# Marking accumulating banks with work that is there anyway, in a one-core attention and mixture-of-experts kernel

## The chip, the cores and the metric

The kernel runs on one core of a Trainium2 chip. A core has a matrix engine (TensorE, PE in the profile, with its weight loads as PEld), a vector engine (VectorE, DVE), an activation engine (ScalarE, ACT), a general engine (GpSimd, POOL) and a queue engine for transfers (SyncE, SP). Each runs its own list of instructions in order; they wait for each other through semaphores. Matrix products land in PSUM, eight banks of 128 partitions by 512 fp32 values. The metric is the device time of one execution in microseconds (us).

## The reference, cut to what matters

Two stages. Cross attention between tokens x and 32 state rows per head gives 8 × (512 + 32) = 4352 rows of 512 values. These go through eight experts, all of them on every row, weighted by a matrix P that a gate and eight rounds of row and column normalisation produce.

```python
def _moe_ref(x, w_gate, w1, w2) -> np.ndarray:
    ...
    logits = x @ w_gate
    logits = logits - logits.max()
    P = np.exp(logits)
    for _ in range(8):
        P /= P.sum(1, keepdims=True) + 1e-09
        P /= P.sum(0, keepdims=True) + 1e-09
        P *= N / E
    out = np.zeros((N, D), dtype=np.float32)
    for e in range(E):
        h = np.maximum(x @ w1[e], 0.0)
        ye = h @ w2[e]
        out += P[:, e:e + 1] * ye
    return out.astype(np.float32)
```

Here D is 512, the hidden width 1024, E is 8.

## The kernel before, in words

**Two parts.** The first 135 us are a list of some 736 small operations (`PLAN`, issued one by one by `issue`): attention, the gate, the normalisation rounds, expert 0 whole, and the start of expert 1. After it comes a loop over `work`, the pairs of expert e = 1 to 7 and row block bi = 0 to 8 (eight blocks of 512 rows, one of 256); the document counts iterations from 0. Iteration 0 is expert 1, block 0, whose hidden layer the list has made already. Nothing is reordered afterwards: every engine takes its instructions as the program text issues them.

**One iteration** is three generators advanced in turns. `layer2(e, bi, i)` makes the second layer of the block. `layer1` of the next block makes its hidden layer in eight pieces: two matmuls of 512 columns into one of four banks (`hps`, pool "h"), a relu by ScalarE, and after the fourth and eighth piece four sums by VectorE (lines 281 to 284). `project`, in some iterations, makes V, the projected first-layer weights, for blocks to come: a "session" of line 235, which starts in the E bank and in one of the two accumulating banks.

**The second layer** multiplies 2 × 2 blocks with seven products in place of eight (Strassen's way, Winograd's form), each of eight matmuls of 256 columns (line 334). The document numbers them 1 to 7 as `layer2` issues them: A; E; B; A; B; E; B, where the letters are PSUM banks. Each but the first is followed by its add: VectorE reads the bank and adds it, weighted by P, to `acc` (line 348, two instructions). Bank B begins as a copy of A by ScalarE (line 363), and products 3, 5 and 7 accumulate onto it. So products 5 and 7 may begin only when VectorE has read what was in the bank before.

**The marker.** Products accumulate onto data that ScalarE wrote. [...] The banks stay the same tiles for the whole loop (`seeds`, used in turns by the iteration's parity).

**Scaling.** `acc` holds expert 0's output unweighted. `weigh` (lines 294 and 296) multiplies a block of rows by its column of P; iteration 0 does the first four row blocks ahead of product 1, on VectorE, ScalarE, VectorE and GpSimd.

**The step counter.** `step()` is called after each turn of `layer2` and each piece of `layer1`; each sixth call advances `load_w` of the next expert by one, from block 1 on. `load_w` issues four weight loads, idles for ten turns, and then makes eight subtractions of weights on VectorE (line 206), which land wherever the counter puts them among the adds and sums. What is left at block 6 is done at once.

The loop's turn:

```python
        for k in range(7):
            next(l2)
            step()
            ...
            for _ in range(pat[k]):
                next(l1, None)
                step()
```

Of the kernel before, what the change touches and what calls it, by code (L numbers as in the profile page):

```python
# [9 lines left out]
FP32 = mybir.dt.float32  # L10
FP16 = mybir.dt.float16
# [37 lines left out]
704V 689P 693P 690P 730P 398V 694A 399P 733P 731V 691A 732A 735A 734A 400V  # L49
""".split()  # L50
ENGINES = {"P": "PE", "V": "DVE", "A": "ACT", "G": "POOL", "D": "DMA", "S": "SPQ", "H": "HOST"}
NT_ = 2
ETX = 0
POOLB = 1
# [47 lines left out]
            slot.users.append(self)  # L102


def issue(ops):
    for step in PLAN:
        op = ops[int(step[:-1])]
        assert all(d.end for d in op.after) and ENGINES[step[-1]] in op.on
        for slot in op.takes:
            slot.ring.taken.append(slot)  # L110
            slot.tile = slot.make()
        op.emit(ENGINES[step[-1]])
        op.end = True
    assert all(op.end for op in ops) and len(PLAN) == len(ops)
# [3 lines left out]
def kernel(  # L118
# [9 lines left out]
    nc = tc.nc  # L128

    B, H, S, D = x.shape  # L130
# [14 lines left out]
    DH = Dm // 2  # L145
# [15 lines left out]
    def bank(shape, dtype, name, tag="bank"):  # L161
        return pools[tag].tile(shape, dtype, name=name, tag=tag)

    aT = persist.tile([128, B, NQ, S], FP16, name="aT")
# [5 lines left out]
    identh = persist.tile([128, 128], FP16, name="identh")  # L170
# [87 lines left out]
    hid = {}  # L258
    late = []
    final = (E - 1, B)  # L260
    seeds = []

    def layer1(e, bi):

        t0, tn = blocks[bi]
        th = tn // 2
        Hm = hpool.tile([128, 2, NJ, S], FP16, name="Hm", tag="Hm")
        sm = hpool.tile([128, 3, NJ, S // 2], FP16, name="sm", tag="sm")
        hid[(e, bi)] = (Hm, sm)
        for j in range(NJ):  # L270
            for i in range(2):
                fb = i * NJ + j
                hps = bank([128, S], FP32, "hps", "h")
                hidden_ps(e, bi, fb, hps[:, :tn])
                nc.scalar.activation(out=Hm[:, i, j, :tn], in_=hps[:, :tn], func=AF.Relu)  # L275
                if j % 2 and i and (e, bi) != final:
                    def sums(jj=ds(j - 1, 2)):
                        a11, a21 = Hm[:, 0, jj, :th], Hm[:, 0, jj, th:tn]
                        a12, a22 = Hm[:, 1, jj, :th], Hm[:, 1, jj, th:tn]
                        s1, s2, s4 = (sm[:, k, jj, :th] for k in range(3))  # L280
                        nc.vector.tensor_add(s1, a21, a22)  # L281
                        nc.vector.tensor_sub(a21, a11, a21)  # L282
                        nc.vector.tensor_sub(s2, s1, a11)  # L283
                        nc.vector.tensor_sub(s4, a12, s2)  # L284

                    if DEFER and bi == 0 and j == 1:
                        late.append(sums)
                    else:
                        sums()
                yield  # L290

    def weigh(k, eng):
        if eng == "ACT":
            nc.scalar.mul(acc[:, k, :], acc[:, k, :], Pmat[:, k, 0:1])
        else:
            (nc.vector if eng == "DVE" else nc.gpsimd).tensor_scalar(
                out=acc[:, k, :], in0=acc[:, k, :], scalar1=Pmat[:, k, 0:1], scalar2=None, op0=ALU.mult)
# [22 lines left out]
    def layer2(e, bi, n):  # L320
        t0, tn = blocks[bi]
        nk = tn // 256
        th = tn // 2
        Hm, sm = hid.pop((e, bi))
        w2h, T = w16[e][1], tsum[e]
        tb = t0 // 128
        p = Pmat[:, :, e:e + 1]
        A = bank([128, 2, DH], FP32, "A", "A")
        Eb = bank([128, 2, DH], FP32, "E", "E")

        def product(dst, lhs, rhs, first=False):
            for c in range(nk):
                for j in range(NJ):
                    nc.tensor.matmul(dst[:, c], lhs(j, c), rhs[:, j],  # L334
                                     start=first and c == 0 and j == 0, stop=(j == NJ - 1),
                                     skip_group_check=True)

        def h(i, half):
            return lambda j, c: Hm[:, i, j, ds(half * th + c * 128, 128)]

        def s(k):
            return lambda j, c: sm[:, k, j, ds(c * 128, 128)]

        def add(src, row, col):
            for c in range(nk):
                k = tb + row * nk + c
                dst = acc[:, k, ds(col * DH, DH)]
                nc.vector.scalar_tensor_tensor(out=dst, in0=src[:, c], scalar=p[:, k], in1=dst,  # L348
                                               op0=ALU.mult, op1=ALU.add)

        def seed(i):
            bb = bank([128, 2, DH], FP32, "Bseed", "B%d" % i)
            nc.tensor.matmul(bb.rearrange("p c d -> p (c d)"), identh, aT[:, 0, 0], start=True, stop=True)
            seeds.append(bb)

        if not n:
            for k, eng in enumerate(("DVE", "ACT", "DVE", "POOL")):
                weigh(k, eng)
        product(A, h(0, 0), w2h[:, :NJ, :DH], True)
        if not n:  # L360
            seed(0)
        Bb = seeds[n % 2]
        nc.scalar.copy(out=Bb[:, :nk], in_=A[:, :nk])  # L363
        yield
        product(Eb, s(0), T[:, 0], True)
        if not n:
            seed(1)
        add(Eb, 1, 1)
        yield
        product(Bb, s(1), T[:, 1])  # L370
        add(Bb, 0, 1)
        yield
        product(A, h(1, 0), w2h[:, NJ:, :DH])
        add(A, 0, 0)
        yield
        product(Bb, h(0, 1), T[:, 2])
        add(Bb, 1, 1)
        yield
        product(Eb, s(2), w2h[:, NJ:, DH:])
        add(Eb, 0, 1)  # L380
        yield
        product(Bb, h(1, 1), T[:, 3])
        add(Bb, 1, 0)
        if e == E - 1 and bi < B:
            for k in range(2 * nk):
                nc.sync.dma_start(out=outx[bi][:, k, :], in_=acc[:, tb + k, :])
        yield


    ops = []  # L390
# [96 lines left out]
    for g in range(4):  # L487
# [10 lines left out]
        t = op((0, 1, g), {"PE": (0.35, 0.55)}, turn, bd[g // 2 * 2:g // 2 * 2 + 2] + [makeh], [ps])  # L498
# [68 lines left out]
    for b in range(B):  # L567
# [5 lines left out]
        for g in range(2 if b < NT else 0):  # L573
# [11 lines left out]
            t = op((due_x(2 * b + g) - 2.0, 0), {"PE": (0.70, 0.88)}, turnX, [x_ready[b][g], makeh], [ps], [xn[b]])  # L585
# [221 lines left out]
    def tile_of(tag, shape):  # L807
# [6 lines left out]
    c = sk({"DVE": (0.36, 0.48)}, lambda: nc.vector.reduce_max(  # L814
        out=tile_of("lmx", [128, 1]), in_=logits.rearrange("p t e -> p (t e)"), axis=AX_X), gates)
    mT = psum([1, 128], FP32, "mT_ps")
    c = sk({"PE": (0.11, 0.35)}, lambda: nc.tensor.transpose(mT.tile, sm_["lmx"], ident32), [c, make32], takes=[mT])
# [3 lines left out]
    c = sk({"PE": (0.18, 0.45)}, lambda: nc.tensor.matmul(gb.tile, ones128[0:1, :], sm_["gm"]), [c], takes=[gb])  # L821
# [193 lines left out]

                op((due_1 + 5.0 * bi, 2, j), {"DVE": (1.70, 1.85)}, sums, kept[-4:]).goal = -0.9

    issue(ops)
    for e in range(2):
        w16[e] = (wslots[e][0].tile, wslots[e][1].tile)  # L1020
    hpool = pools1["h"]
# [6 lines left out]
    n = 0  # L1028

    def step():  # L1030
        nonlocal n
        n += 1
        if n % 6 == 0 and wload:
            try:
                next(wload[0])
            except StopIteration:
                wload.pop(0)
# [4 lines left out]
    for i, (e, bi) in enumerate(work):  # L1042
        if bi == 1 and e + 1 < E:
            wload.append(load_w(e + 1))
        if (e, bi) == final:
            layer2_last()
            break
        v, pat = iter(()), PATS if bi == B else PATN if bi == B - 1 else PAT0
        soon = work[:i + (3 if bi == B - 1 else 2)]
        need = sum(b < B for _, b in soon) * (F // 512)  # L1050
        if halves and all_halves - len(halves) < need:
            v, pat = project(halves[:SESSION], i), PATV
            del halves[:SESSION]
        if i:
            next(v, None)
        l2 = layer2(e, bi, i)
        l1 = layer1(*work[i + 1]) if i + 1 < len(work) and work[i + 1] not in hid else iter(())
        for k in range(7):
            next(l2)
            step()  # L1060
            if k == 0:
                next(v, None)
                next(v, None)
            if late:
                late.pop()()
            if e == 1 and bi < B and 3 <= k < 7:
                m = blocks[bi + 1][0] // 128 + k - 3
                if m < NTB:
                    weigh(m, "ACT")
# [3 lines that stand above are left out]
        for part in (l1, l2):  # L1073
            for _ in part:
                pass
        if bi == len(blocks) - 3:
            for _ in (x for w in wload for x in w):
                pass
            wload.clear()
# [30 lines left out]
```

## Time and profile before

| | |
|---|---|
| median of 3 runs | 752.74 us (752.53 to 753.22) |
| profiled execution | 752.75 us |
| its span, first to last instruction | 751.0 us |
| granted TensorE clock, mean over the span | 0.995 |
| PE busy | 736.0 us (98%) |
| DVE busy | 617.0 us (82%) |
| ACT busy | 517.7 us (69%) |
| POOL busy | 70.8 us (9%) |
| chain that ended last: PE / DVE | 92% / 3% |
| products of the second layer (line 334) in the chain | 48% |
| first-layer pieces (line 255) in the chain | 28% |

The span is cut into what each engine does; busy shares overlap. The chain is followed back from the last instruction, at each step to what released it, so its shares add up to the span. A matmul's length in a row includes its way through the array, and the next one starts before it ends; what one costs is read from start to start.

### The profile page before, as it was taken

Reading aid. Unit: us, or ns where it says so; the run is one execution under the profiler, and the core shown is the slowest. Engines: PE = TensorE matmul, PEld = TensorE weight load, DVE = VectorE, ACT = ScalarE, POOL = GpSimd, SP = SyncE. Lnnn points to the kernel's source line nnn. Section 1 sums busy time; section 2 is a strip of 40 time slices with the busy share of each in tenths; the row PEclk is TensorE's granted clock in tenths of the full one; section 3 lists DMA queues with packets and bytes.
Section 4 is the critical chain, followed back from the end, with each engine's and each line's share of the span. In section 5 each row is a group of like instructions: output and inputs, shape, how many; then the busy total and the mean of one; then the engine's idle time right before and its main releaser. Section 6 shows DMA issues by size and latency. Waiting matters only on the chain.

```text
span 751.0 us, 16151 instructions
## 1 busy us (share of the span) xinstructions
PE 736.0 (98%) x6517; PEld 502.2 (67%) x6517; DVE 617.0 (82%) x1529; ACT 517.7 (69%) x1014; POOL 70.8 (9%) x81
## 2 busy tenths in 40 slices
PE   5999999999999999999999999999999999999997
PEld 3444445666777777776776767776777767767776
DVE  5899989877888789788888788887897888887885
ACT  6876856799876766667666766667666676667662
POOL 4674410200010000100000000100001000000000
PEclk9899999999999999999999999999999999999999
DMA  9997560600033000700007000330007000002234
GB/s 179 140 134 131 82 99 1 109 6 1 1 61 53 2 1 2 113 1 2 1 2 112 2 1 1 58 57 1 1 2 112 2 1 2 1 31 94 103 113 141
DMA packets 51323, 36.71 MB, mean 49 GB/s; under 512 B 25392, under 2 KB 43824, under 8 KB 51248
## 3 DMA queue, kind: packets, MB, share of 16 engines
q0 software_dynamic: 22272, 20.97, 18.5%
q1 hardware_dynamic: 27744, 14.18, 7.6%
q8 instruction: 51, 0.84, 0.5%
q10 hardware_dynamic: 1232, 0.52, 0.3%
q14 instruction: 24, 0.20, 0.1%
HBM read 42.48 MB, written 8.91 MB: 68 GB/s over the span
## 4 chain that ended last, share of the span: by engine, by line
PE 92%; DVE 3%; DMA 1%; ACT 1%; POOL 1%; issue 0%; SPq 0%; POOLq 0%; DVEq 0%; ACTq 0%
PE hps L255 28%; PE Bseed L334 20%; PE A L334 14%; PE E L334 14%; PE yps L935 6%; PE hps L897 4%; PE v_ps L235 4%; DMA xT<-x_nat 1%; DMA x_nat<-in_x_dram 1%; PE y L312 0%; PE v_ps L870 0%; POOL a L670 0%; ACT Hm L275 0%; DVE acc L348 0%; POOL E L662 0%; PE su_ps L758 0%
## 5 line engine op out<-in xcount | busy, mean ns | idle before, releaser
L275 ACT ACTIVATE Hm<-hps 128x512 f16<-128x512 f32 (+1 forms) x496 | 265.8, 577 | 130.5 <-PE hps L255 128.1
L255 PE MATMUL hps<-aT,V 128*128 128x512 f16 x880 | 230.6, 379 | 0.0
L334 PEld LDWEIGHTS <-Hm 128*128 128x128 f16 x1888 | 181.6, 98 | 71.3 <-issue 15.9
L348 DVE SCALAR_TENSOR_TENSOR acc<-Bseed,Pmat,acc 128x256 f32<-128x256 f32 x354 | 155.0, 477 | 9.8 <-PE Bseed L334 6.9
L334 PEld LDWEIGHTS <-sm 128*128 128x128 f16 x1416 | 138.3, 98 | 34.5 <-issue 0.3
L334 PE MATMUL A<-w2h,Hm 128*128 128x256 f16 x944 | 123.7, 273 | 0.0
L334 PE MATMUL Bseed<-T,Hm 128*128 128x256 f16 x944 | 123.3, 273 | 0.0
L255 PEld LDWEIGHTS <-V 128*128 128x128 f16 x880 | 86.1, 98 | 50.8
L348 DVE SCALAR_TENSOR_TENSOR acc<-E,Pmat,acc 128x256 f32<-128x256 f32 x236 | 103.2, 476 | 13.8 <-PE E L334 13.5
L281 DVE TENSOR_TENSOR sm<-Hm 128x512 f16<-128x512 f16 (+1 forms) x122 | 50.1, 411 | 60.4 <-ACT Hm L275 60.2
L243 ACT CAST V<-v_ps 128x512 f16<-128x512 f32 x144 | 74.2, 612 | 0.0
L348 DVE SCALAR_TENSOR_TENSOR acc<-A,Pmat,acc 128x256 f32<-128x256 f32 x118 | 51.9, 479 | 17.9 <-PE A L334 17.6
L935 PE MATMUL yps<-w2h,hT 128*128 128x512 f16 x272 | 64.1, 379 | 0.1
L334 PE MATMUL E<-w2h,sm 128*128 128x256 f16 x472 | 61.7, 273 | 0.0
L334 PE MATMUL E<-T,sm 128*128 128x256 f16 x472 | 61.6, 273 | 0.0
L334 PE MATMUL Bseed<-T,sm 128*128 128x256 f16 x472 | 61.5, 272 | 0.0
L363 ACT COPY Bseed<-A 128x512 f32<-128x512 f32 (+1 forms) x62 | 34.1, 550 | 37.9 <-PE A L334 35.3
L282 DVE TENSOR_TENSOR Hm<-Hm 128x512 f16<-128x512 f16 (+1 forms) x122 | 50.3, 412 | 4.2
L284 DVE TENSOR_TENSOR sm<-Hm,sm 128x512 f16<-128x512 f16 (+1 forms) x122 | 50.2, 412 | 4.2
L283 DVE TENSOR_TENSOR sm<-sm,Hm 128x512 f16<-128x512 f16 (+1 forms) x122 | 49.4, 405 | 0.0
L194 POOL DMA_DIRECT2D w1h<-in_moe_w_dram x12 | 8.5, 714 | 396.9 <-PE hps L255 396.5
L935 PEld LDWEIGHTS <-hT 128*128 128x128 f16 x272 | 25.4, 99 | 28.9 <-issue 1.8
(127 smaller groups left out, 617.7 us busy)
## 6 DMA issues: line engine op xcount, KB each, us to landing
w1h<-in_moe_w_dram POOLq DMA_DIRECT2D x16, 512.0 KB, 7.0
w2h<-in_moe_w_dram POOLq DMA_DIRECT2D x16, 512.0 KB, 8.4
out_dram<-acc SPq DMA_DIRECT2D x32, 256.0 KB, 2.5
x_nat<-in_x_dram POOLq DMA_DIRECT2D x16, 256.0 KB, 5.6
st_st<-in_state_dram ACTq DMA_DIRECT2D x1, 256.0 KB, 4.9
st_st<-in_state_dram SPq DMA_DIRECT2D x1, 256.0 KB, 4.2
ETs<-E SPq DMA_TRANSPOSE x16, 4.3
out_dram<-acc SPq DMA_DIRECT2D x4, 64.0 KB, 1.8
```

The source lines that it names most:

```text
L235: nc.tensor.matmul(ps[q][ds(j * Ns, Ns), :], stT[ds(r, 64), bi, q, ds((j ^ q) * Ns, Ns)], w1h[ds(r, 64), 2 * q + j // 2, cols], tile_posit ...
L243: nc.scalar.copy(out=dst, in_=src)
L255: nc.tensor.matmul(out, lhs, rhs, start=(k == 0), stop=(k == len(terms) - 1))
L275: nc.scalar.activation(out=Hm[:, i, j, :tn], in_=hps[:, :tn], func=AF.Relu)
L281: nc.vector.tensor_add(s1, a21, a22)
L282: nc.vector.tensor_sub(a21, a11, a21)
L283: nc.vector.tensor_sub(s2, s1, a11)
L284: nc.vector.tensor_sub(s4, a12, s2)
L334: nc.tensor.matmul(dst[:, c], lhs(j, c), rhs[:, j], start=first and c == 0 and j == 0, stop=(j == NJ - 1), skip_group_check=True)
L348: nc.vector.scalar_tensor_tensor(out=dst, in0=src[:, c], scalar=p[:, k], in1=dst, op0=ALU.mult, op1=ALU.add)
L363: nc.scalar.copy(out=Bb[:, :nk], in_=A[:, :nk])
L935: nc.tensor.matmul(yps.tile, hT[fb].tile[:, ds(tk * 128, 128)], w2h[:, fb, :], start=(fb == 0), stop=(fb == NFB - 1))
```

## The change

Iteration 0 no longer issues the two markers. The first B bank is lent to the first piece of the next block's hidden layer, which is therefore issued right behind product 1, ahead of product 2; the relu reads it from there, and then ScalarE copies A over it. The second B bank is first written by the projection session of iteration 1. ScalarE's scaling of row block 1 moves behind its copy of A, and VectorE scales row block 2 before row block 0. The turn that issues the lent piece calls `step()` once more. `issue` gets a hook for idle matmuls with an empty table.

```diff
+IDLE = {}
...
-def issue(ops):
+def issue(ops, idle):
...
+        idle(op.takes[0].tile if op.takes else None, IDLE.get(int(step[:-1]), 0))
...
-    def layer1(e, bi):
+    def layer1(e, bi, lent=None):
...
-                hps = bank([128, S], FP32, "hps", "h")
+                if lent is None:
+                    hps = bank([128, S], FP32, "hps", "h")
+                else:
+                    hps, lent = lent, None
...
-        def seed(i):
-            bb = bank([128, 2, DH], FP32, "Bseed", "B%d" % i)
-            nc.tensor.matmul(bb.rearrange("p c d -> p (c d)"), identh, aT[:, 0, 0], start=True, stop=True)
-            seeds.append(bb)
-
         if not n:
-            for k, eng in enumerate(("DVE", "ACT", "DVE", "POOL")):
+            for k, eng in ((2, "DVE"), (3, "POOL"), (0, "DVE")):
                 weigh(k, eng)
         product(A, h(0, 0), w2h[:, :NJ, :DH], True)
+        Bb = seeds[n % 2]
         if not n:
-            seed(0)
-        Bb = seeds[n % 2]
+            yield
         nc.scalar.copy(out=Bb[:, :nk], in_=A[:, :nk])
+        if not n:
+            weigh(1, "ACT")
         yield
         product(Eb, s(0), T[:, 0], True)
-        if not n:
-            seed(1)
         add(Eb, 1, 1)
...
+        if not i:
+            seeds += [bank([128, 2, DH], FP32, "Bseed", "B%d" % k) for k in range(2)]
         l2 = layer2(e, bi, i)
-        l1 = layer1(*work[i + 1]) if i + 1 < len(work) and work[i + 1] not in hid else iter(())
+        l1 = iter(())
+        if i + 1 < len(work) and work[i + 1] not in hid:
+            l1 = layer1(*work[i + 1], None if i else seeds[0].rearrange("p c d -> p (c d)"))
+        if not i:
+            next(l2)
+            next(l1)
+            step()
         for k in range(7):
             next(l2)
             step()
```

More of the change, by code (lines that the diff above doesn't have):

```diff
@@ L1016, with idle @@
                 op((due_1 + 5.0 * bi, 2, j), {"DVE": (1.70, 1.85)}, sums, kept[-4:]).goal = -0.9
-    issue(ops)
+    def idle(t, n):
+        if not n:
+            return
+        t = t.rearrange({2: "p a -> p a", 3: "p a b -> p (a b)", 4: "p a b c -> p (a b c)"}[len(t.shape)])[:, :128]
+        for _ in range(n):
+            if t.dtype == FP16:
+                nc.tensor.transpose(t, identh, identh)
+            else:
+                nc.tensor.matmul(t, identh, identh, start=True, stop=True, skip_group_check=True)
+    issue(ops, idle)
     for e in range(2):
```

## The prediction

> **What bounds the kernel now.** First the page's head and its chain of waits: which engine sets the end.
>
> ```profile
> PE 736.0 (98%) x6517; PEld 502.2 (67%) x6517; DVE 617.0 (82%) x1529; ACT 517.7 (69%) x1014; POOL 70.8 (9%) x81
> ...
> PE 92%; DVE 3%; DMA 1%; ACT 1%; POOL 1%; issue 0%; SPq 0%; POOLq 0%; DVEq 0%; ACTq 0%
> ```
>
> TensorE carries 92% of the chain, and from 135 us on it is never idle (77.00 of 77.00 us busy in the stretch 135 to 212). There a microsecond counts only if TensorE issues less, or has to wait. So next the timeline of the loop's first iteration, where the edit lies. Columns: start, length, engine, line, operation, tiles.
>
> ```profile
> 134.73 1.62 ACT L419 CAST V<-v_ps 128x512 f16<-128x512 f32 x3
> 135.14 1.05 PE L334 MATMUL A<-w2h,Hm 128*128 128x256 f16 x8
> 136.03 0.38 PE L353 MATMUL Bseed<-aT,identh 128*128 128x512 f16 x1
> 136.24 0.73 ACT L294 ACTIVATE acc<-acc,Pmat 128x512 f32<-128x512 f32 x1
> 136.41 1.03 PE L334 MATMUL E<-T,sm 128*128 128x256 f16 x8
> 136.86 0.60 ACT L363 COPY Bseed<-A 128x512 f32<-128x512 f32 x1
> 137.28 0.38 PE L353 MATMUL Bseed<-aT,identh 128*128 128x512 f16 x1
> 137.49 0.59 PE L255 MATMUL hps<-aT,V 128*128 128x512 f16 x2
> 137.93 1.04 PE L334 MATMUL Bseed<-T,sm 128*128 128x256 f16 x8
> ```
>
> Starts, not lengths, give TensorE's cost: eight matmuls of 256 columns take 0.87 us (139.23 to 140.10 in the same timeline), four of 512 columns 0.87 us (140.10 to 140.97), so 0.217 us each. A marker thus costs 0.217 us, not 0.38. After the first marker TensorE also waits: product 2 could start at 136.25 but does at 136.41, just behind the last eviction of V (134.73 + 1.62 = 136.35).
>
> Last the timeline of a later iteration with a subtraction of load_w (line 206) in it:
>
> ```profile
> 545.89 0.42 DVE L284 TENSOR_TENSOR sm<-Hm,sm 128x512 f16<-128x512 f16 x1
> 546.24 0.87 DVE L348 SCALAR_TENSOR_TENSOR acc<-Bseed,Pmat,acc 128x256 f32<-128x256 f32 x2
> 546.30 1.03 PE L255 MATMUL hps<-aT,V 128*128 128x512 f16 x4
> ...
> 547.02 0.41 DVE L206 TENSOR_TENSOR T<-w2h 128x512 f16<-128x512 f16 x1
> 547.16 1.04 PE L334 MATMUL Bseed<-T,Hm 128*128 128x256 f16 x8
> 547.36 0.87 DVE L348 SCALAR_TENSOR_TENSOR acc<-E,Pmat,acc 128x256 f32<-128x256 f32 x2
> 548.14 0.41 DVE L281 TENSOR_TENSOR sm<-Hm 128x512 f16<-128x512 f16 x1
> 548.28 0.37 PE L235 MATMUL v_ps<-w1h,stT 64*32 64x512 f16 x1
> ```
>
> Product 7 accumulates into the bank that VectorE has just read for product 5's add (line 348). That add ends at 547.11 and product 7 starts at 547.16: VectorE has no room here. The same holds at the projection session (line 235), which takes the E bank: the E add ends at 548.22, the session starts at 548.28.
>
> **The change part by part.** It has two effects, and the second is not visible in the diff's words.
>
> (1) The first iteration. Two markers leave, 0.43 us of TensorE. Piece 1 takes the first one's place: two matmuls from 136.03 to 136.46. It needs the first half of V (evicted by 135.31), not the last. Product 2 follows at 136.46, past the 136.41 that held it, so this wait (0.16 us) goes too; it ends at 137.33, piece 2 at 137.77. Now product 3 waits for ScalarE: piece 1's second matmul starts 136.25 and lasts 0.38, to 136.63; the relu starts some 0.07 later (after a piece ends it took 0.04 and 0.11 here) and lasts 0.60, to 137.30; the copy of A overwrites the bank the relu read, so it starts at about 137.35 and lasts 0.57 to 0.60. Product 3 starts at about 137.97, 0.04 later than before, but one piece (0.43 us) is already done. Net −0.39. What is late next would be product 5 or 7, but the fourth piece and its sums come 0.4 us earlier too, so nothing new binds. Ends: −0.59 (both markers and the wait go, ScalarE hides) and −0.07 (piece 1 has to wait for V's last eviction, product 3 at 138.3).
>
> ScalarE's scaling (0.73 us) now stands behind its copy; queued behind it is the relu of piece 2, ending about 139.2. Its bank is asked for again by piece 6, near 141.9, and the scaled row by VectorE's second add of product 3, near 139.5: no cost. VectorE scales block 2 before block 0 (the E add wants 2 first, at 137.6): no cost. GpSimd's scaling stays first on its queue, and the weight loads behind it wait for buffers, 396.5 us in all, not for the loop's program order: no cost. The idle hook issues nothing, its table being empty; the built program has two matmuls fewer on TensorE, so the markers do leave.
>
> (2) The step counter. The first iteration now calls step() 16 times, not 15, and every sixth call drives load_w. From there on each subtraction of line 206 is put one step earlier on VectorE. In the built program's order 24 of the 48 get another neighbour. Of these, 12 pass an add that nobody is short of (product 5 starts 0.75 us or more behind product 3's add where this happens; the bank that product 7's add reads is wanted again two iterations later).
>
> Six (before: 196.01, 293.94, 370.94, 468.94, 547.02, 645.11) go from behind product 5's add to ahead of it, behind the sums of lines 281 to 284. Price of one subtraction in a VectorE queue that is full: four in a row, whose rows start at 297.43 and whose follower starts at 298.77, 1.34 / 4 = 0.335 us.
>
> ```profile
> 297.43 0.75 DVE L206 TENSOR_TENSOR T<-w2h 128x512 f16<-128x512 f16 x2
> 298.10 0.75 DVE L206 TENSOR_TENSOR T<-w2h,T 128x512 f16<-128x512 f16 x2
> 298.77 0.87 DVE L348 SCALAR_TENSOR_TENSOR acc<-E,Pmat,acc 128x256 f32<-128x256 f32 x2
> ```
>
> I take 0.325, since the step from a sum to the subtraction replaces one to the add (0.35). Product 7 starts this much later, less its room over the 0.05 release: the add ended 0.12 before product 7 at 371.14 and 469.14, 0.05 to 0.06 at the other four. So 2 × 0.26 and 4 × 0.32 = 1.80. But four of these iterations precede a session which today already waits for the E add that this subtraction delays: its first matmul comes 0.289, 0.290, 0.347, 0.344 us after the last, against 0.203 where there is no wait, 0.46 in all. The E add ends as before, TensorE now arrives later, so this wait is absorbed: 1.80 − 0.46 = +1.34.
>
> Six others (206.28, 284.28, 382.31, 460.22, 558.39, 635.39) go from behind the E add to ahead of it. A session follows at four (206.67, 284.61, 382.64, 635.78), where the E add ends 0.31, 0.24, 0.25 and 0.30 before it. The same subtraction in the same place cost the session 0.087 where the room was 0.3 and 0.143 where it was 0.25 (the four excesses above): 2 × 0.087 + 2 × 0.143 = +0.46. The other two feed product 2, which has over 0.6 us of room.
>
> Sum: −0.39 + 1.34 + 0.46 = +1.41. The profiled execution took 752.75 (span 751.0 and 1.75 around it), like the median, 752.74. So 754.16, call it 754.2: +0.19%.
>
> [...] The row says 0.335 from start to start, though one lasts 0.415. [...]
>
> **The rivals.** *The subtractions are hidden* (not slower). At four of the six places product 7 starts exactly one matmul slot, 0.216 us, behind the piece before it, so TensorE is not seen waiting there; if product 7 had 0.33 us of room that the release shows wrongly, only part 1 would count: 752.4. Against it: in the ScalarE-loaded iterations at 154.98, 165.51, 185.61 and 196.14 product 7 is 0.09 late, 0.05 behind the same add; it does bind. It decides from a room of about 0.25 us.
>
> *Full price.* If a subtraction between a sum and a PSUM add holds the queue for its 0.415 us, the six cost 1.89 after absorption and the four sessions 0.16 or 0.23 each, 0.77: −0.39 + 1.89 + 0.77 = +2.27, 755.0. It decides at once: 0.01 us more at each of the ten places crosses the line of 0.2% below. For it: no row shows a subtraction between a sum and an add that reads PSUM. Against: the 0.335.
>
> *The first iteration gains nothing.* Relu and copy now stand in series before product 3; if piece 1 is held to 136.41, −0.07 instead of −0.39: 754.5. For it: the whole V tile is read by later pieces; against: piece 1 reads columns of the first half alone.
>
> *The marks cost nothing and the shift helps*: subtractions leave the E add in four iterations; without any price at product 7, −0.39 − 0.46 = −0.85: 751.9, still not 0.2%.
>
> **How the numbers follow.** Forecast 0.70 (its own range 753.8 to 754.6: 0.05 us on each of ten stalls, partly together, and 0.2 on part 1); hidden 0.09; full price 0.09; no gain at the front 0.09; shift helps 0.03. 0.2% is 1.5 us, about what a measurement of this kernel can tell from no change: the line lies at 754.25, almost on the forecast. Of the forecast 0.29 lies above it and 0.41 below. Slower: 0.29, with full price and nearly all of the third case 0.17 more, 0.46. Faster: 0.02, what the last case holds with luck beyond −1.5. Same: the rest, 0.52. The range 753.3 to 755.1 leaves out the first and the last rival (0.12) and some 0.05 at the ends.
>
> **What would show it.** Right: no line-353 markers; product 3 near 138.0 and product 7 of the first iteration near 144.05; from there a constant lead of 0.39 until about 196; then product 7 late by 0.26 to 0.32 in one iteration per expert 1 to 6, with a line-206 row between line 284's and the add; sessions near 206, 284, 382 and 635 later by 0.09 or 0.14, while those near 372, 470, 548 and 646 no longer wait. Wrong: product 7 on time behind such a row; a price near 0.42; product 3 past 138.2.

## The result, and the profile after

| | before | after |
|---|---|---|
| median of 19 runs each, us | 752.97 (751.01 to 755.71) | 755.27 (753.81 to 756.44) |
| ratio, with 95% interval | | 1.0029 [1.0021, 1.0036] |
| profiled execution, us | 752.75 | 753.84 |
| its span, us | 751.0 | 752.1 |
| start of product 1 of iteration 0, us | 135.14 | 134.31 |
| the loop: from there to the span's end, us | 615.83 | 617.75 |

The change made the kernel slower by 0.29%, or 2.18 us (0.0029 × 752.97, interval 1.58 to 2.71). The forecast was 754.2, a difference of +1.41, with a range up to 755.1, so the time lies just above the range. The two profiled executions differ by 1.1 us only. The reason is that the 135 us ahead of the loop are not the same from one execution to the next: in the eleven profiles of this document, product 1 starts anywhere from 134.16 to 135.92. The loop, which holds the whole difference, is far steadier, and it is 1.92 us longer. So this document compares loops, and takes the time of the kernel from the medians.

First the chain of waits of the kernel after, from its page, with the page's row for the products that accumulate in a B bank.

```profile
PE 89%; DVE 5%; ACT 3%; DMA 2%; POOL 1%; issue 1%; SPq 0%; POOLq 0%; ACTq 0%; DVEq 0%
...
L339 PE MATMUL Bseed<-T,Hm 128*128 128x256 f16 x944 | 123.3, 273 | 1.0 <-DVE acc L353 0.7
```

TensorE's share fell from 92% to 89%, VectorE's rose from 3% to 5%: the chain now leaves TensorE at places where product 7 waits for an add. The row says so too. Before, its idle column was 0.0; now it is 1.0 us, of which 0.7 ended with line 353 (the add, 348 before). That is less than half of what these waits cost (1.84 us, below), because idle time is counted from the modelled end of the matmul before, and a matmul's row is longer than its slot (product 2 in the timeline below has a row of 1.04 us, and piece 2 starts 0.87 behind it). Steps from start to start show all of it.

The timeline of iteration 0 after the change (columns: start, length, engine, line, operation, tiles; line 339 is a product, 257 a piece, 280 its relu, 363 the copy of A, 299 the scaling):

```profile
133.90 1.62 ACT L419 CAST V<-v_ps 128x512 f16<-128x512 f32 x3
...
134.31 1.05 PE L339 MATMUL A<-w2h,Hm 128*128 128x256 f16 x8
...
135.20 0.59 PE L257 MATMUL Bseed<-aT,V 128*128 128x512 f16 x2
...
135.63 1.04 PE L339 MATMUL E<-T,sm 128*128 128x256 f16 x8
135.83 0.60 ACT L280 ACTIVATE Hm<-Bseed 128x512 f16<-128x512 f32 x1 [0.30 <-PE Bseed L257]
136.46 0.57 ACT L363 COPY Bseed<-A 128x512 f32<-128x512 f32 x1
136.50 0.59 PE L257 MATMUL hps<-aT,V 128*128 128x512 f16 x2
...
136.94 0.72 ACT L299 ACTIVATE acc<-acc,Pmat 128x512 f32<-128x512 f32 x1
137.08 1.03 PE L339 MATMUL Bseed<-T,sm 128*128 128x256 f16 x8
...
143.16 1.04 PE L339 MATMUL Bseed<-T,Hm 128*128 128x256 f16 x8
```

No marker is left: before, they were two matmuls of the identity into the B banks, at 136.03 and 137.28, whose result nobody used. The first matmul into a B bank is now piece 1 for one and, at 144.13, the session for the other; that one has to come ahead of ScalarE's first copy is a premise of the kernel which no run shows. Piece 1 starts at 135.20, ahead of the end of V's last eviction (135.52). Product 3 starts 2.77 us behind product 1 (137.08 − 134.31), against 2.79 before, with one piece more already done. Product 7 starts 8.85 us behind product 1; before it was 9.30. So the front of the loop is 0.45 us shorter, and the rest of it, from product 7 of iteration 0 to the end, went from 606.53 to 608.90 us: 2.37 us longer.

The timeline at iteration 41, the place that the prediction showed of before (208 is the subtraction, 286 to 289 the sums, 237 the session):

```profile
546.28 0.42 DVE L289 TENSOR_TENSOR sm<-Hm,sm 128x512 f16<-128x512 f16 x1
546.62 0.42 DVE L208 TENSOR_TENSOR T<-w2h 128x512 f16<-128x512 f16 x1
546.69 1.03 PE L257 MATMUL hps<-aT,V 128*128 128x512 f16 x4
546.95 0.87 DVE L353 SCALAR_TENSOR_TENSOR acc<-Bseed,Pmat,acc 128x256 f32<-128x256 f32 x2
...
547.74 0.86 DVE L353 SCALAR_TENSOR_TENSOR acc<-E,Pmat,acc 128x256 f32<-128x256 f32 x2
547.88 1.03 PE L339 MATMUL Bseed<-T,Hm 128*128 128x256 f16 x8 [0.16 <-DVE acc L353]
548.52 0.41 DVE L286 TENSOR_TENSOR sm<-Hm 128x512 f16<-128x512 f16 x1
548.84 0.39 PE L237 MATMUL v_ps<-w1h,stT 64*32 64x512 f16 x1
```

The subtraction now stands between the last sum and product 5's add. The add starts 0.33 later (546.95 instead of 546.62, where the subtraction stands), and with it product 7. This is the mechanism that was forecast, at its place.

What no step of the prediction has is in iteration 29. Its copy of A (line 363) starts late. The timeline before:

```profile
420.42 1.05 PE L334 MATMUL A<-w2h,Hm 128*128 128x256 f16 x8
420.60 0.59 ACT L240 CAST V<-Bseed 128x512 f16<-128x512 f32 x1
...
421.56 0.57 ACT L363 COPY Bseed<-A 128x512 f32<-128x512 f32 x1 [0.36 <-PE A L334]
...
422.18 1.03 PE L334 MATMUL Bseed<-T,sm 128*128 128x256 f16 x8
```

and after:

```profile
420.34 1.05 PE L339 MATMUL A<-w2h,Hm 128*128 128x256 f16 x8
420.52 0.59 ACT L242 CAST V<-Bseed 128x512 f16<-128x512 f32 x1
...
421.77 0.57 ACT L363 COPY Bseed<-A 128x512 f32<-128x512 f32 x1 [0.66 <-PE A L339]
...
422.39 1.03 PE L339 MATMUL Bseed<-T,sm 128*128 128x256 f16 x8
```

The same product, the same eviction of V in front, and yet the copy begins 1.43 us behind product 1 (421.77 − 420.34) instead of 1.14 (421.56 − 420.42); ScalarE is idle ahead of it for 0.66 instead of 0.36. Product 3, the last row shown, waits for that copy. Iteration 56 has the same, 1.42. The step from the matmul before to product 3 is 0.405 us in iteration 29 and 0.391 in iteration 56; in the kernel before it is 0.113 at both places.

The loop, put together from steps between starts:

| part | forecast, us | measured, us |
|---|---|---|
| front of iteration 0 (product 1 to product 7) | −0.39 | −0.45 |
| product 7 late in iterations 5, 15, 23, 33, 41, 51 | +1.80 | +0.338 + 0.320 + 0.267 + 0.265 + 0.324 + 0.325 = +1.84 |
| waits of sessions 24, 34, 42, 52 that go | −0.46 | −0.46 |
| new waits of sessions 7, 15, 25, 51 | +0.46 | +0.085 + 0.139 + 0.143 + 0.080 = +0.45 |
| product 3 late in iterations 29, 56, behind the copy | none | +0.292 + 0.278 = +0.57 |
| sum | +1.41 | +1.95; the loop shows 617.75 − 615.83 = +1.92 |

The rows account for the loop's difference to 0.03 us, so nothing else of size is in it.

### The profile page after: what moved, and what is told of

It reads as the page before. It is cut to its first block, busy times and chain, and to the rows that moved or that the text cites. A ratio compares the mean times of both kernels' runs of the same rounds, so it can differ in the third digit from the quotient of the medians.

```text
span 752.1 us, 16146 instructions
## 1 busy us (share of the span) xinstructions
PE 735.9 (98%) x6515; PEld 501.9 (67%) x6515; DVE 616.3 (82%) x1529; ACT 518.0 (69%) x1014; POOL 70.8 (9%) x81
## 4 chain that ended last, share of the span: by engine, by line
PE 89%; DVE 5%; ACT 3%; DMA 2%; POOL 1%; issue 1%; SPq 0%; POOLq 0%; ACTq 0%; DVEq 0%
PE hps L257 26%; PE Bseed L339 20%; PE A L339 14%; PE E L339 12%; PE yps L935 7%; PE hps L897 4%; PE v_ps L237 4%; ACT Hm L280 2%; DVE acc L353 1%; DMA xT<-x_nat 1%; DMA x_nat<-in_x_dram 1%; PE v_ps L870 0%; DVE sm L286 0%; PE y L317 0%; DVE sm L289 0%
```

## The experiments

In each, "loop" is the time from product 1 of iteration 0 to the span's end in the profiled execution; ratios are to the kernel before, timed on the same chip.

Two explanations of the late copies were to be told apart from the start. By the one they are a further result of the step counter, some other order of VectorE or TensorE. By the other they come from ScalarE's own list of instructions. In the built program that list has 1162 instructions before and 1161 after: the relu of the first piece had to wait for two engines before, one of the waits as an instruction of its own; it reads the B bank now, and one wait is enough. So every later instruction of ScalarE has a number lower by one. The late copies are numbers 689 and 1073 of the list after, which lie 3 × 128 apart; in the list before, the semaphore instruction just ahead of each copy had these numbers. The traces agree: with the instructions that stand around the program they show 1176 and 1175 of ScalarE, the one that is gone is the relu's semaphore instruction at 138.12, and the late copies are numbers 704 and 1088 there.

### The change once more

The kernel after, unchanged, to see whether the late copies stay where they are.

> The changed kernel once more. Loop here means product 1 of iteration 0 to the last instruction: 615.83 us in the kernel before, 617.75 in the changed one. Theory (places are fixed by the program): loop 617.75 again within 0.1, product 7 late in iterations 5, 15, 23, 33, 41, 51, and ScalarE's copy of A late by 0.29 in iterations 29 and 56, at the same two places. Rival (the two late copies were an accident of one execution, a transfer or the like): they are gone or elsewhere, loop 617.2 to 617.8.

Measured: 755.26 us, ratio 1.0032 [1.0020, 1.0044], loop 617.76. The six late products 7, the four sessions and the two copies (iterations 29 and 56) are all there again, within 0.015 us each. Whatever delays the copies is a property of the program, not a chance event.

### Without the additional step

```diff
         if not i:
             next(l2)
             next(l1)
-            step()
```

> The changed kernel without the additional step() in iteration 0; the lent piece and the moved scaling stay. Theory: the subtractions return to their old neighbours, product 7 waits nowhere beyond iterations 1, 2, 4, 5, sessions wait in 24, 34, 42, 52 as before; the two late copies in 29 and 56 stay, as ScalarE's list is unchanged: loop 617.75 - 1.80 = 615.95. Rival (the lent piece itself or the moved scaling makes the later iterations late): loop stays at 617.7.

Measured: 753.0 us, ratio 1.0001 [0.9992, 1.0010], loop 615.93. Its timeline at iteration 41:

```profile
545.81 0.42 DVE L289 TENSOR_TENSOR sm<-Hm,sm 128x512 f16<-128x512 f16 x1
546.15 0.87 DVE L353 SCALAR_TENSOR_TENSOR acc<-Bseed,Pmat,acc 128x256 f32<-128x256 f32 x2
546.22 1.03 PE L257 MATMUL hps<-aT,V 128*128 128x512 f16 x4
...
546.94 0.41 DVE L208 TENSOR_TENSOR T<-w2h 128x512 f16<-128x512 f16 x1
547.08 1.04 PE L339 MATMUL Bseed<-T,Hm 128*128 128x256 f16 x8
```

The subtraction is back behind the add, product 7 starts 0.14 behind it and waits no more; sessions 24, 34, 42 and 52 have their old waits again. The two late copies stay. So the one call of `step()` makes 617.75 − 615.93 = 1.82 us of the loop (1.84 − 0.46 + 0.45 = 1.83 by rows), and the copies have nothing to do with it. They also explain why this kernel is no faster than before: its front gains 0.45, its copies lose 0.57.

### The additional step alone

Against the kernel before, with its markers:

```diff
+        if not i:
+            step()
         for k in range(7):
```

> The kernel before with one additional step() ahead of iteration 0 and nothing else. Theory: six late product 7 and four late sessions as in the changed kernel, no late copies: loop 615.83 + 1.80 = 617.63. Rival (it needs the lent piece): 615.83.

Measured: 755.47 us, ratio 1.0035 [1.0020, 1.0050], loop 617.66. The same six products and the same four sessions are late, no copy is. Together with the run before, this is the step's price from both sides: +1.82 and +1.83. It also shows that the front and the copies together come to no gain: the kernel after has a loop of 617.75, this one 617.66.

### One more instruction for ScalarE, at the very start

A copy of one column into a tile that nobody reads, behind the warm-up activation of the list. It gives every later ScalarE instruction its old number back.

```diff
+    spare_ = spl.tile([128, 1], FP32, name="spare_")
+
+    def warming(_):
+        nc.scalar.activation(out=warm, in_=warm, func=AF.Exp)
+        for f in range(1):
+            nc.scalar.copy(out=spare_[:, f:f + 1], in_=warm)
```

> The changed kernel with one more ScalarE instruction (a copy of one column) at the very start, so that every later ScalarE instruction stands at the number that it had before the change (the change took one semaphore instruction off ScalarE's list). Theory (the two late copies come from where ScalarE's list is cut into pieces as it is fetched): both copies on time, the rest as changed: loop 617.75 - 0.57 = 617.18. Rival (late copies come from the moved subtractions or from a transfer): still 617.75.

Measured: 754.59 us, ratio 1.0024 [1.0015, 1.0033], loop 617.22. Iteration 29 in its timeline:

```profile
421.69 1.05 PE L339 MATMUL A<-w2h,Hm 128*128 128x256 f16 x8
421.87 0.59 ACT L242 CAST V<-Bseed 128x512 f16<-128x512 f32 x1
...
422.83 0.57 ACT L363 COPY Bseed<-A 128x512 f32<-128x512 f32 x1 [0.37 <-PE A L339]
```

The copy starts 1.14 behind product 1, as before the change. One instruction added some 400 us earlier takes 0.53 us out of the loop. The late copies hang on an instruction's number in ScalarE's list.

### Three more instead of one

The same edit with three columns and three copies. If the number is what matters, other copies have to be late: those whose number is now 128 times something behind 689.

> The changed kernel with three more ScalarE instructions at the very start in place of one. Theory: a cut comes after each 128 instructions of ScalarE's list (the two late copies stand at numbers 689 and 1073, 3 x 128 apart); with three more, the copies of iterations 11 and 38 stand at that place of a cut (433 and 817), so these two are late by 0.29 and those of 29 and 56 are not: loop 617.2 + 0.57 = 617.8. Rival (any additional ScalarE instruction at the start helps, whatever its number): no late copy, loop 617.2.

Measured, in a single execution and so without an interval: 754.21 us, loop 617.88. The copies of iterations 29 and 56 are on time; those of iterations 11 and 38 are late, by the same amount (step to product 3 0.392 each). Their numbers are 433 and 817. Iteration 38:

```profile
508.82 0.59 ACT L242 CAST V<-Bseed 128x512 f16<-128x512 f32 x1
...
510.05 0.57 ACT L363 COPY Bseed<-A 128x512 f32<-128x512 f32 x1 [0.65 <-PE A L339]
```

ScalarE idles 0.65 ahead of it, as in iteration 29 after the change. Four numbers, 433, 689, 817 and 1073, all leave 49 when divided by 128.

### Two steps in place of one

The counter starts at 1, so that everything it drives comes one step earlier still.

```diff
-    n = 0
+    n = 1
```

> The changed kernel with the step counter starting at 1, so that from iteration 0 on it is two steps ahead of the kernel before, not one. Theory (only the subtractions' places count): none stands between the sums and product 5's add any more, sessions wait in 7, 15, 25, 51 in place of 24, 34, 42, 52; the two late copies stay: loop 615.83 - 0.46 + 0.46 - 0.46 + 0.57 = 615.94. Rival (each step ahead costs): 619 or more.

Measured, in a single execution: 751.9 us, loop 615.97. No product 7 is late beyond those of before; sessions 7, 15, 25 and 51 are, and the copies of iterations 29 and 56. The difference to the kernel after, 617.75 − 615.97 = 1.78, is the six products alone (1.84 by rows). So the cost is one of phase: a subtraction right ahead of product 5's add is dear, one place further along it is not. It is no cost of "one step more" as such.

### Both causes taken out

After, without the additional step and with one instruction more for ScalarE.

> The changed kernel without the additional step() and with the one ScalarE instruction more: what is left of the change is the lent piece, the markers gone and the scaling moved. Theory: loop 615.83 - 0.46 = 615.37, as fast as the kernel before by the median within 0.2%. Rival (part of the gain comes from elsewhere): 615.8.

Measured: 752.38 us, ratio 0.9992 [0.9982, 1.0002], loop 615.40, which is 0.43 under the kernel before (615.83). This is the front's gain by itself (0.45 by rows). A gain of 0.06% is too small for the medians to show; the interval holds it, and zero.

### Subtractions placed by hand

As the run before, but `load_w` is no longer driven by the counter: the loads go out at block 1, and two subtractions each stand behind product 4's add in blocks 4 to 7.

```diff
-        for _ in range(10):
-            yield
+        yield
...
-        if n % 6 == 0 and wload:
-            try:
-                next(wload[0])
-            except StopIteration:
-                wload.pop(0)
+        pass
...
-            wload.append(load_w(e + 1))
+            wload[:] = [load_w(e + 1)]
+            next(wload[0])
...
+            if k == 3 and wload and 4 <= bi < 8:
+                for _ in range(2):
+                    next(wload[0], None)
...
-        if bi == len(blocks) - 3:
-            for _ in (x for w in wload for x in w):
-                pass
-            wload.clear()
```

> As the one before, but load_w no longer goes by the step counter: its loads are issued at block 1, and two subtractions at a time are put behind product 4's add in blocks 4 to 7, where VectorE idled 0.34 to 1.2 us before the sums. Theory: no session waits for a subtraction and no product 7 either: loop 615.37 - 0.46 = 614.91. Rival (two in a row outlast the idle time, or the weights land late): 615.4 or more.

Measured: 751.88 us, ratio 0.9988 [0.9977, 0.9999], loop 614.92. VectorE's timeline at iteration 41 (lines are one lower in this kernel):

```profile
542.35 0.88 DVE L352 SCALAR_TENSOR_TENSOR acc<-A,Pmat,acc 128x256 f32<-128x256 f32 x2 [0.36 <-PE A L338]
543.14 0.75 DVE L207 TENSOR_TENSOR T<-w2h,T 128x512 f16<-128x512 f16 x2
544.39 0.42 DVE L285 TENSOR_TENSOR sm<-Hm 128x512 f16<-128x512 f16 x1 [0.49 <-ACT Hm L279]
```

Two subtractions run behind the add of bank A, and VectorE still idles 0.49 us before the next sum: there the place is free. No session waits any more, and 615.40 − 614.92 = 0.48 is the four old session waits (0.46). This version is faster than both kernels, though by only 0.12% against before, with an interval that ends just below 1.

### ScalarE's scaling ahead of its copy

Against after, the scaling of row block 1 stands ahead of the copy of A again, to see what the third part of the change was worth.

```diff
-        nc.scalar.copy(out=Bb[:, :nk], in_=A[:, :nk])
         if not n:
             weigh(1, "ACT")
+        nc.scalar.copy(out=Bb[:, :nk], in_=A[:, :nk])
```

> The changed kernel with ScalarE's scaling of row block 1 put back ahead of its copy of A; everything else as changed. Theory: the scaling (0.72 us, 0.49 to 0.64 from start to start) stands between the relu and the copy that product 3 waits for, so product 3 of iteration 0 starts 0.49 to 0.64 later, 3.3 us behind product 1 in place of 2.77, and the loop takes 617.76 + 0.55 = 618.3; the lent piece without the moved scaling would then lose what it gains. Rival (product 3 has other cover): 617.76.

Measured, in a single execution: 755.69 us, loop 618.31. In iteration 0:

```profile
137.12 0.60 ACT L280 ACTIVATE Hm<-Bseed 128x512 f16<-128x512 f32 x1 [0.30 <-PE Bseed L257]
137.61 0.71 ACT L299 ACTIVATE acc<-acc,Pmat 128x512 f32<-128x512 f32 x1
...
138.22 0.59 ACT L365 COPY Bseed<-A 128x512 f32<-128x512 f32 x1
...
138.86 0.38 PE L339 MATMUL Bseed<-T,sm 128*128 128x256 f16 x2 [0.48 <-ACT Bseed L365]
```

Product 3 starts 3.26 behind product 1 (which starts at 135.60) instead of 2.77, and product 7 starts 9.34 behind it instead of 8.85, so all of the 0.49 arrives. With a piece lent the bank, the copy stands behind the relu; a scaling in between would have used up the whole gain of leaving the markers out. The prediction costed that move at nothing as a step of its own, and did not say that the gain hangs on it.

## Why the prediction missed

**Iteration 0: right, −0.45 for −0.39.** The order relu, copy, product 3 and the reason why piece 1 does not wait (it needs the first half of V) are what the timeline shows. The copy started 2.15 behind product 1, where 2.21 was worked out; that is the 0.06 of difference. The rival that nothing is gained here is refuted by product 3 at 2.77 and by the loop of 615.40 with both other causes taken out.

**The step counter: right, +1.83 for +1.80.** All ten places were named, and the two runs with the step alone and without it give +1.83 and +1.82. Product 7 was forecast 0.26 late in iterations 23 and 33 and 0.32 in the other four; it was 0.265, 0.267, and 0.320 to 0.338. The sessions were forecast at 0.087 and 0.143; they were 0.080 to 0.085 and 0.139 to 0.143. A price that is read where the same instruction stands in the same kind of place carries over to a few hundredths of a microsecond.

**The rivals on the price: refuted.** "Hidden" would have left product 7 where it was. "Full price" gave 755.0, close to the median of 755.27, yet for a reason that the trace refutes: a subtraction between a sum and the add costs 0.33 (546.62 to 546.95), not its length of 0.42. The next operation begins some 0.08 us before the subtraction's row ends, whether it reads PSUM, as here, or not, as in the four in a row of the prediction (0.415 long, 0.335 from start to start). "Shift helps" fell with the first rows. A total that agrees is no proof of its terms.

**The step that failed** is the sentence "It has two effects, and the second is not visible in the diff's words", and the sum −0.39 + 1.34 + 0.46 built on it. There is a third: one semaphore instruction fewer on ScalarE, and by it two copies late at 0.29 and 0.28, +0.57 us. "Nothing new binds" was looked at for iteration 0 alone. With this term the sum is 1.98 and the time 754.7 from the same base. What remains up to 755.27 is 0.23 that the base moved (752.74 over 3 runs, 752.97 over 19), and some 0.3 between medians of times that spread over 2.6 us and more; the interval of the difference, 1.58 to 2.71, holds the 1.95 of the rows and not the 1.41 of the prediction. The range itself, up to 755.1, would have held 754.7: it was left only because the missing term and the 0.55 of base and scatter came together.

Could the third effect have been seen? That ScalarE's list had become shorter by one could be counted in the built program. That this costs something, no copy in the trace of before shows. There the copies of iterations 20 and 47 had the numbers 561 and 945, which also leave 49 when divided by 128, and they started on time, 1.07 behind product 1. So the mistake to learn from is one of width: the sum had terms only for what the edit names, and the range had only the bounds of those terms.

## What to carry to other kernels

A call that is added to a shared counter moves everything which the counter drives: look for work that is placed by counting, not only for what the diff names, and cost each moved instruction at its new neighbours. Filler work belongs behind an instruction whose result nobody is short of, placed by hand, where a shift elsewhere can't move it. When a small change is measured in a kernel whose first part scatters, compare the stretch that holds the difference, from a common start, and sum up the late steps in it until they account for all of it.

## What the hardware showed that was not expected

**An instruction's number can cost 0.29 us.** ScalarE's copy of A is late when its number leaves 49 divided by 128 and a semaphore instruction that waits for product 1 stands just ahead of it, in an iteration with a session before. It is late by the same amount in iterations 29 and 56 of four kernels, and in 11 and 38 when three instructions are put in front; one instruction in front removes it. In iterations 20 and 47 of the kernel before, without a session just ahead, the same number cost nothing. That it goes with the number is shown. Is it the fetching of the list? The page has two instruction queues: one moved 51 packets and 0.84 MB, some 16.5 kB each, the other 24 packets and 0.20 MB, some 8.3 kB each. The trace shows how far ScalarE is when packets of the second queue start: in the kernel before, six of them start at 246.62, 332.31, 421.42, 510.13, 595.99 and 685.15, when 448, 575, 703, 832, 959 and 1087 of the 1176 instructions that the trace shows of it have started, 127 to 129 apart. The eight others between them start when 567 to 1464 of VectorE's have started, 126 to 130 apart. The late numbers 689 and 817 are 128 apart too.

The time of a packet moves with the number. Near iteration 29 a packet of the second queue starts at 421.42 in the kernel before, 0.14 us ahead of the copy, and at 422.69 in the kernel after, 0.92 us behind the copy's start. For all twelve late copies of the profiles it starts 0.64 to 0.92 us behind the copy's start. For the copies of iterations 29 and 56 in the five kernels where they have their old number, it starts between 0.42 us ahead and 0.09 us behind. So the fetching moves with the number, and with the lateness. But a late copy does not wait for that packet, which starts only after it, so what holds the copy for 0.29 us stays open, and that the fetch is the cause remains inferred. In iterations 20 and 47 of the kernel before the packet starts 0.75 us ahead of the copy, while ScalarE sits idle for 1.09 us until product 1 is ready. That a delay is hidden in this idle time fits these rows; no run tested it.

**The part ahead of the loop scatters more than the effect.** In eleven profiles of ten programs that differ little there, product 1 of the loop started at 134.16 to 135.92 us, 1.8 us apart; the loops of the kernel after, profiled twice, agree within 0.02 us (617.75 and 617.76). One profiled execution against another would have shown 1.1 us for this change, the loops 1.92, the medians 2.3.
